# Attention scores of two heads: four small matmuls against a block-diagonal product, and four more units masked by TensorE

## The chip, the cores and the metric

The program runs on one core of one Trainium2 chip. The metric is the device time of one execution in microseconds (us). Before the change the median of three runs is 630.11 us (627.29 to 633.33). One more execution was profiled; its own time is 631.83 us, and its trace spans 630.1 us.

## The reference

Sliding-window causal attention feeds a mixture of experts that picks one expert for each token. All data is fp32.

```
B, H, S, DH = 8, 8, 576, 64          # 4608 tokens, 8 heads
scores = (q @ k^T) / sqrt(DH)        # a query sees itself and the 63 keys before it
attn   = softmax(where(0 <= rel < 64, scores, -1e9))
x      = (attn @ v) as (B, S, H*DH)  # D = 512
logits = x @ w_gate                  # E = 8 experts, F = 1024
e      = argmax(logits), or the expert of the token before where sigmoid(x @ w_local) >= 0.5
out    = softmax(logits)[e] * (relu(x @ w1[e]) @ w2[e])
```

## The kernel before, in words

**Stages.** `attention` computes x, stores it to DRAM (`xs`, L547) and computes the gate's logits on the way. `Router` works out which tokens go to which expert. `Experts.run` then takes blocks of up to 256 tokens of one expert, gathers their rows and does the two products. The Router's first part is woven into the end of attention, its second part into the first expert blocks.

**Tiling of the attention.** The 4608 tokens are nine superchunks (`sc`, 512 tokens each), the heads are four pairs (`hp`). A unit is one (sc, hp): 36 units. Head j of a pair lies on partitions 64j to 64j+63, for queries as for keys. Keys go in blocks of 64 (`WIN`), eight in a superchunk. A query sees the keys of its own block and of the one before, so each key block meets 128 queries. `scores` (L387) puts the scores of even key blocks of the superchunk on partitions 0 to 63 of a PSUM bank (c = 0) and those of the odd ones on partitions 64 to 127 (c = 1), one bank `sp[j]` for each head, 512 queries wide. Each product (L394) takes 64 rows (one head), 64 columns (64 keys) and 128 queries, or 64 at the ends. A quarter of the array holds it; the four quarters (two heads, two values of c) take turns in the code. An fp32 product appears twice in the trace, so that the 18 products of a unit are 36 matmuls and 36 weight loads there.

**What follows the scores.** ScalarE takes exp of each bank into `p` (L425), VectorE multiplies `p` with a mask (L430), except in the units in `BIASED`: there TensorE first writes a large negative number to the masked places (`bias`, `never`, L409, bf16) and adds the scores to it. `values` (L433) does 16 fp32 products (L440): 128 rows, which are the keys of two blocks, 64 columns of queries, and 65 (74 from superchunk 4 on) values of one head. VectorE divides by the sum (L445, L450).

**What sets the order.** TensorE, ScalarE and SP follow the order of the code. In the loop over the units (L479) the scores run two units ahead (`LEAD`): the body emits the scores of unit i+2, then copies of values for the next superchunk (`shift`), transposes or gate products, then the values of unit i. GpSimd and VectorE are placed by a scheduler.

**Loads.** Queries and keys lie together in DRAM (`kq`). One tile of a ring of four (`ring`, 16 KB a partition) holds both for one superchunk. `load(sc + 3, pairs)` at hp = 1 (L533) issues two DMAs of 1 MB from SP; the ring makes the first wait until the scores of superchunk sc are done. Values (`va`) are loaded two superchunks ahead at hp = 0, transposed values (`vtt`) at hp = 2. Later the same ring holds the experts' weights w1 and w2.

## Time and profile before

| what | us |
|---|---|
| median of three runs | 630.11 |
| profiled execution, its own time | 631.83 |
| its span | 630.1 |
| attention's last values begin | 133.31 |
| first expert products begin | 134.50 |

PE is the matmuls, PEld the weight loads that run beside them, DVE is VectorE, ACT ScalarE, POOL GpSimd, SP the engine that issues the loads. The profile's table of 40 slices shows PE at 70 to 90 per cent until some 110 us, and at 90 per cent or more from there nearly to the end, so that the kernel has two parts to read: the attention, in which PE has gaps, and the experts, in which it has next to none. The DMA engines show eight tenths or more in the first nine slices. Idle time of an engine that nobody waits for costs nothing, so a row says something about the time only where PE stands behind it.

### The profile page before, as it was taken

How to read it: one execution, taken by the hardware profiler on the slowest of the kernel's cores; microseconds unless marked ns; L12 is line 12 of the kernel's file. 1: busy time of each engine (PE TensorE's matmuls, PEld its weight loads, DVE VectorE, ACT ScalarE, POOL GpSimd, SP SyncE). 2: the span in 40 equal slices, each digit the busy share in tenths (PEclk: the TensorE clock that was granted, in tenths of full speed). 3: DMA queues.
4: the chain of work that ended last, by engine and by line, in shares of the span. 5: the costliest groups of instructions: out<-in, count | busy, mean ns of one | idle time of the engine just before them, and what ended most of it. 6: DMA issues, size and time to landing. Idle time of an engine off the chain costs nothing. (4 is left out here: it accounts for less than half of the span.)

```text
span 630.1 us, 15072 instructions
## 1 busy us (share of the span) xinstructions
PE 604.0 (96%) x6253; PEld 530.7 (84%) x6253; DVE 402.1 (64%) x757; ACT 200.7 (32%) x368; POOL 275.5 (44%) x261
## 2 busy tenths in 40 slices
PE   8897988999999999999999999999999999999995
PEld 7676766788889998979898889888997998989994
DVE  5667569888986867346472785183927753886730
ACT  3756655632482131203130213022211221213120
POOL 4532111532103567448165873174375765462001
PEclk9999999999999999999999999999999999999998
DMA  8999898886945566487966765678678656965501
GB/s 319 397 419 400 326 377 298 287 319 238 384 154 202 185 227 250 165 295 248 403 244 236 304 221 208 225 305 318 284 262 320 225 186 240 374 217 208 197 18 39
DMA packets 31880, 165.80 MB, mean 263 GB/s; under 512 B 10531, under 2 KB 12217, under 8 KB 22586
## 3 DMA queue, kind: packets, MB, share of 16 engines
q1 hardware_dynamic: 20394, 135.54, 57.9%
q0 software_dynamic: 11408, 29.20, 13.0%
q8 instruction: 51, 0.84, 0.5%
q14 instruction: 27, 0.22, 0.1%
HBM read 145.52 MB, written 19.59 MB: 262 GB/s over the span
## 5 line engine op out<-in xcount | busy, mean ns | idle before, releaser
L1184 POOL DMA_INDIRECT xg<-xs,g x118 | 139.1, 1179 | 46.5 <-issue 25.6
L1488 POOL DMA_INDIRECT out_dram<-y,idx x36 | 40.8, 1133 | 159.0 <-DVE y L1419 69.9
L1408 PE MATMUL hp<-ws,hs 128*128 128x256 f32 x384 | 88.9, 380 | 0.0
L1408 PEld LDWEIGHTS hp<-ws,hs 128*128 128x128 f32 x384 | 72.6, 190 | 10.9 <-issue 1.2
L1357 PE MATMUL hp<-xs,ws 128*128 128x128 f32 x672 | 79.7, 275 | 0.0
L1357 PEld LDWEIGHTS hp<-xs,ws 128*128 128x128 f32 x672 | 77.3, 192 | 0.1
L1508 PE MATMUL hp<-xt,w 128*64 128x64 f32 (+2 forms) x640 | 66.2, 276 | 0.0
L1508 PEld LDWEIGHTS hp<-xt,w 128*128 128x128 f32 (+1 forms) x640 | 60.8, 170 | 4.1 <-issue 0.7
L1419 DVE SCALAR_TENSOR_TENSOR y<-hp,pws,kept 128x256 f32<-128x256 f32 x48 | 22.1, 480 | 63.5 <-issue 38.1
L1408 PE MATMUL hp<-w,h 128*128 128x256 f32 x256 | 60.5, 379 | 0.0
L1369 DVE TENSOR_TENSOR h<-hp,keep 128x512 f32<-128x512 f32 x42 | 28.6, 690 | 44.0 <-PE hp L1357 43.2
L1357 PEld LDWEIGHTS hp<-xt,w 128*128 128x128 f32 x448 | 53.2, 192 | 2.7 <-issue 2.3
L1357 PE MATMUL hp<-xt,w 128*128 128x128 f32 x448 | 54.7, 275 | 0.0
L394 PEld LDWEIGHTS sp<-w 64*64 64x64 f32 x1296 | 39.9, 139 | 16.1 <-issue 11.5
L1408 PEld LDWEIGHTS hp<-w,h 128*128 128x128 f32 x256 | 47.3, 190 | 5.7
L394 PE MATMUL sp<-w 64*64 64x128 f32 (+1 forms) x1296 | 45.8, 272 | 5.7 <-issue 4.2
L425 ACT ACTIVATE p<-sp 128x512 f32<-128x512 f32 x72 | 39.1, 595 | 37.6 <-PE sp L394 35.2
L440 PE MATMUL xo<-vb,p 128*64 128x74 f32 (+1 forms) x576 | 45.0, 230 | 5.5 <-DVE x L450 2.2
L430 DVE TENSOR_TENSOR p<-p,mask 128x1024 f32<-128x1024 f32 x29 | 35.6, 1227 | 22.6 <-ACT p L425 22.5
L1184 POOL DMA_INDIRECT pws<-xw,gx x40 | 43.7, 1093 | 13.1 <-issue 9.8
L440 PEld LDWEIGHTS xo<-vb,p 128*64 128x64 f32 x576 | 39.2, 139 | 9.7 <-issue 4.0
L1320 DVE TENSOR_TENSOR ws<-w 128x1024 f32<-128x1024 f32 x32 | 39.1, 1224 | 11.5 <-PE hp L1408 9.6
(287 smaller groups left out, 967.3 us busy)
## 6 DMA issues: line engine op xcount, KB each, us to landing
w<-in_w_dram SPq DMA_DIRECT2D x22, 2048.0 KB, 9.4
w<-in_w1t_dram SPq DMA_DIRECT2D x20, 2048.0 KB, 8.9
w<-in_kq_dram SPq DMA_DIRECT2D x17, 1024.0 KB, 10.4
w<-in_w_dram SPq DMA_DIRECT2D x24, 512.0 KB, 8.3
xs<-x POOLq DMA_DIRECT2D x9, 1024.0 KB, 7.0
va<-in_v_dram SPq DMA_DIRECT2D x5, 1184.0 KB, 5.3
vtt<-in_vt_dram SPq DMA_DIRECT2D x5, 1024.0 KB, 6.3
va<-in_v_dram SPq DMA_DIRECT2D x3, 1040.0 KB, 14.2
```

Of the source, the lines that this page charges most:

```text
L394: nc.tensor.matmul(sp[j][c * WIN:(c + 1) * WIN, a:b], lhsT=kt[h, hp, block * WIN:(block + 1) * WIN], rhs=qt[h, hp, a:b], start=not biased, ...
L425: nc.scalar.activation(p[:, j], sp[j], Act.Exp, scale=DH ** -0.5)
L430: masked.append(nc.vector.tensor_tensor(p, p, m.to_broadcast([P, 2, SC]), op=Alu.mult))
L440: nc.tensor.matmul(xo[par * WIN:(par + 1) * WIN, j, s * VW:s * VW + n], lhsT=p[:, j, b * WIN:(b + 1) * WIN], rhs=w[:, s, 2 * hp + j, :n], ...
L1184: return self.nc.gpsimd.indirect_dma_start(out=out, out_offset=None, in_=table[:rows, :], in_offset=bass.IndirectOffsetOnAxis(ap=idx, axis=0))
L1320: self.nc.vector.tensor_tensor(o, x, y, op=sub)
L1357: mm = nc.tensor.matmul(out[:, m, :], lhsT=a[:, kk, m * P:(m + 1) * P], rhs=b[:, kk, :], start=start and m + kk == 0, stop=stop and (m, kk ...
L1369: nc.vector.tensor_tensor(o, x, y, op=add)
L1408: mm = nc.tensor.matmul(out, lhsT=a[:, m, :], rhs=b[:, m, :], start=start and m == 0, stop=stop and m == FK // 2 - 1, skip_group_check=True)
L1419: nc.vector.scalar_tensor_tensor(o, x, pw[i], y2, Alu.mult, Alu.add)
L1488: return self.nc.gpsimd.indirect_dma_start(out=self.out[:, :], out_offset=bass.IndirectOffsetOnAxis(ap=st["idx"][:, s:s + 1], axis=0), in_ ...
L1508: mm = nc.tensor.matmul(hp[a, i, :], lhsT=st["w1"][:, kk, m * P:(m + 1) * P][:, a], rhs=st["xt"][:, kk, :n], start=(kk == 0), stop=(kk == ...
```

## The change

- **Scores.** The queries of a pair of heads go into a tile whose second axis is the head: head 0's queries on partitions 0 to 63 at place 0, head 1's on partitions 64 to 127 at place 1, and zeros elsewhere. One product takes the keys of both heads (128 rows, 64 keys) and streams the queries of both places (2 x 128). The zeros keep the heads apart. A unit has 10 products, not 18. A bank `sp[i]` now holds both heads for one half (256 queries) of the superchunk, and exp goes by halves.
- **Masks.** (7, 1), (7, 3), (8, 0) and (8, 2) join `BIASED`: 11 units get their mask from TensorE, 25 from VectorE. The bias products take one half of the queries and write it for both heads.
- **Loads.** The ring is two tiles `w1` and two tiles `w2`. Keys: one `w1` tile holds two superchunks, the last superchunk's keys have a tile of their own. Queries: the two `w2` tiles take turns for even and odd superchunks, and their zeros are written once (`clear`). Queries are loaded two superchunks ahead, a pair of `hp` at a time, in two DMAs of 64 partitions each; the first two of all are issued by ScalarE. The experts' weights use `w1` and `w2` in the same turns.

TensorE, the scores of the unit (0, 2) and the first values after them, before. `sp` is the scores' bank, `w` the tile with keys and queries, `xo` the output of the values; the sizes are rows and streamed elements.

```order
L394 MATMUL sp<-w 64x128 x2
L394 MATMUL sp<-w 64x64 x2
L394 MATMUL sp<-w 64x128 x12
L394 MATMUL sp<-w 64x64 x2
L440 MATMUL xo<-vb,p 64x65
L440 MATMUL xo<-va,p 64x65
```

The same place now; `w_129` holds queries and `w_138` keys.

```order
L417 MATMUL sp<-w_129,w_138 64x2x128
L417 MATMUL sp<-w_129,w_138 64x2x64
L417 MATMUL sp<-w_129,w_138 64x2x128 x2
L417 MATMUL sp<-w_129,w_138 64x2x64 x2
L417 MATMUL sp<-w_129,w_138 64x2x128 x3
L417 MATMUL sp<-w_129,w_138 64x2x64
L465 MATMUL xo<-vb,p 64x65
L465 MATMUL xo<-va,p 64x65
```

The unit's 18 products have become 10; six of them stream 2 x 128 queries and four 2 x 64. The place among the other work is the same.

SP's loads from superchunk 2's first unit to the next superchunk's, before, with what each waits for (`DMAHW` is the landing of an earlier load, `PE` a matmul):

```order
L235 DMA va<-in_v_dram 128x2368 [waits PE_49,DMAHW3_49,Activation_49,Pool_49]
L240 DMA w<-in_kq_dram 128x2048 [waits DMAHW4_49,PE_49]
L240 DMA w<-in_kq_dram 128x2048 [waits DMAHW5_49]
L230 DMA vtt<-in_vt_dram 128x2048 [waits DMAHW6_49]
L235 DMA va<-in_v_dram 128x2368 [waits PE_49,DMAHW7_49,Activation_49,Pool_49]
```

The same stretch now:

```order
L246 DMA va<-in_v_dram 128x2368 [waits PE_49,DMAHW1_49,Activation_49,Pool_49]
L259 DMA w_129<-in_kq_dram 64x1024 [waits DMAHW2_49]
L259 DMA w_129<-in_kq_dram 64x1024 [waits DMAHW3_49]
L254 DMA w_785<-in_kq_dram 128x2048 [waits DMAHW4_49,PE_49]
L259 DMA w_129<-in_kq_dram 64x1024 [waits DMAHW5_49,PE_49]
L259 DMA w_129<-in_kq_dram 64x1024 [waits DMAHW6_49]
L241 DMA vtt<-in_vt_dram 128x2048 [waits DMAHW7_49]
L254 DMA w_785<-in_kq_dram 128x2048 [waits DMAHW0_49]
L246 DMA va<-in_v_dram 128x2368 [waits PE_49,DMAHW1_49,Activation_49,Pool_49]
```

Two loads of a superchunk's keys and queries, three superchunks ahead, have become four of queries (two superchunks ahead) and two of keys (here for superchunks 4 and 5).

The diff, without the lines on the experts' ring and the later paths:

```diff
-BIASED = [(4, 3), (5, 1), (5, 3), (6, 0), (6, 1), (6, 2), (6, 3)]
+BIASED = [(4, 3), (5, 1), (5, 3), (6, 0), (6, 1), (6, 2), (6, 3), (7, 1), (7, 3), (8, 0), (8, 2)]
...
-        ring = fast.enter_context(tc.tile_pool(name="ring", bufs=4))
+        ring = fast.enter_context(tc.tile_pool(name="ring", bufs=2))
...
+    turns = [ring.tile([P, 2, 2, 2, SC], F32, name="w2") for _ in range(2)]
+    turns.reverse()
+    for sc in range(NSC):
+        qts[sc] = turns[sc % 2]
+
+    def clear(sc, pair, hps, engines):
+        for j, e in enumerate(engines):
+            e.memset(qts[sc][j * DH:(j + 1) * DH, pair, 1 - j, hps], 0.0)
+
+    clear(0, 0, slice(0, 1), (nc.gpsimd, nc.vector))
...
             else:
-                if sc not in kqs:
-                    kqs[sc] = ring.tile([P, HP, 2, SC], F32, name="w")
-                    kts[sc], qts[sc] = kqs[sc][:, :, 0], kqs[sc][:, :, 1]
-                nc.sync.dma_start(out=kqs[sc][:, part], in_=kq[sc, :, part])
+                pair, hps = part if isinstance(part, list) else (part, slice(0, 2))
+                for j in range(2):
+                    h, e = slice(j * DH, (j + 1) * DH), nc.scalar if (sc, pair, hps.stop) == (0, 0, 1) else nc.sync
+                    e.dma_start(out=qts[sc][h, pair, j, hps],
+                                in_=kq[sc, h, 1, 2 * pair + hps.start:2 * pair + hps.stop])
...
-    load(0, [slice(0, 1), slice(1, 2), (0, H // 2), pairs[1], (H // 2, H)])
+    load(0, [[0, slice(0, 1)], slice(0, 1), slice(1, 2), [0, slice(1, 2)], (0, H // 2), pairs[1], 1, (H // 2, H)])
...
+    clear(0, 0, slice(1, 2), (nc.gpsimd, nc.vector))
+    clear(0, 1, slice(0, 2), (nc.gpsimd, nc.gpsimd))
+    clear(1, 0, slice(0, 2), (nc.gpsimd, nc.gpsimd))
...
     def scores(sc, hp):
-        qt, kt = qts[sc], kts[sc]
-        sp = [ps_s.tile([P, SC], F32, name="sp") for _ in range(2)]
+        qt, kt, half = qts[sc][:, hp // 2, :, hp % 2], kts[sc], SC // 2
+        sp = [ps_s.tile([P, 2, half], F32, name="sp") for _ in range(2)]
...
-        def one(j, c, kt, block, a, b):
-            h = slice(j * DH, (j + 1) * DH)
-            nc.tensor.matmul(sp[j][c * WIN:(c + 1) * WIN, a:b], lhsT=kt[h, hp, block * WIN:(block + 1) * WIN],
-                             rhs=qt[h, hp, a:b], start=not biased, stop=True, skip_group_check=biased)
+        def one(c, kt, block, a, b):
+            i = a // half
+            nc.tensor.matmul(sp[i][c * WIN:(c + 1) * WIN, :, a - i * half:b - i * half],
+                             lhsT=kt[:, hp, block * WIN:(block + 1) * WIN], rhs=qt[:, :, a:b],
+                             start=not biased, stop=True, skip_group_check=biased)
...
-                        nc.tensor.matmul(sp[j][c * WIN:(c + 1) * WIN, a], lhsT=unit[h], rhs=x, start=not n, stop=False,
-                                         skip_group_check=True)
-        for s in range(5):
-            for c in range(2):
-                for j in range(2):
-                    if c == 0:
-                        if s < 4:
-                            one(j, 0, kt, 2 * s, s * P, (s + 1) * P)
-                    elif s:
-                        one(j, 1, kt, 2 * s - 1, s * P - WIN, min(s * P + WIN, SC))
-                    elif sc:
-                        one(j, 1, kts[sc - 1], KB - 1, 0, WIN)
-                    else:
-                        one(j, 1, kt, 1, 0, WIN)
+                            a, w, x = first * WIN - i * half, WIN, never[h]
+                        nc.tensor.matmul(sp[i][c * WIN:(c + 1) * WIN, :, a:a + w], lhsT=unit[h],
+                                         rhs=x.rearrange("p (o q) -> p o q", o=1).to_broadcast([DH, 2, w]),
+                                         start=not n, stop=False, skip_group_check=True)
+        for b in range(KB):
+            if b % 2 == 0:
+                one(0, kt, b, b * WIN, (b + 2) * WIN)
+            lo = b * WIN
+            if b == 0:
+                one(1, *((kts[sc - 1], KB - 1) if sc else (kt, 1)), 0, WIN)
+            elif b % 2 and (lo + WIN) % half:
+                one(1, kt, b, lo, lo + 2 * WIN)
+            elif b % 2:
+                one(1, kt, b, lo, lo + WIN)
+                if b + 1 < KB:
+                    one(1, kt, b, lo + WIN, lo + 2 * WIN)
         p = pp.tile([P, 2, SC], F32, name="p")
-        for j in range(2):
-            nc.scalar.activation(p[:, j], sp[j], Act.Exp, scale=DH ** -0.5)
+        for i in range(2):
+            nc.scalar.activation(p[:, :, i * half:(i + 1) * half], sp[i], Act.Exp, scale=DH ** -0.5)
...
         if 0 < sc < NSC - 2 and hp == 0:
-            load(sc + 2, [whole])
-        if 0 < sc < NSC - 3 and hp == 1:
-            load(sc + 3, pairs)
+            load(sc + 2, [whole, 0])
+        if sc and sc % 2 == 0 and sc + 2 < NSC and hp == 1:
+            load(sc + 2, [slice(0, HP)])
+        if 0 < sc < NSC - 2 and hp == 2:
+            load(sc + 2, [1])
         if hp == 2 and sc + 2 in GATED:
             load(sc + 2, ["turned"])
+        if sc and sc % 2 == 0 and sc + 3 < NSC and hp == 3:
+            load(sc + 3, [slice(0, HP)])
```

More of the change, by code (lines that the diff above doesn't have):

```diff
@@ L148 @@
             with ExitStack() as slow:
-                ring = slow.enter_context(tc.tile_pool(name="ring2", bufs=4))
+                ring = slow.enter_context(tc.tile_pool(name="ring2", bufs=2))
                 rt = Router(slow, tc, lt, xs, tabs, ident)
@@ L160 @@
         with tc.If(if_more > 0), ExitStack() as slow:
-            ring = slow.enter_context(tc.tile_pool(name="ring3", bufs=4))
+            ring = slow.enter_context(tc.tile_pool(name="ring3", bufs=2))
             Experts(slow, tc, ring, *moe).more(slow)
@@ L211, in attention @@
     ctx.enter_context(tc.manual_schedule(engines={ET.PE, ET.Activation, ET.SP}))
-    kqs, qts, kts, vts, vas, vbs = {}, {}, {}, {}, {}, {}
+    qts, kts, vts, vas, vbs = {}, {}, {}, {}, {}
+    turns = [ring.tile([P, 2, 2, 2, SC], F32, name="w2") for _ in range(2)]
[6 more added lines that the diff above has]
+    clear(0, 0, slice(0, 1), (nc.gpsimd, nc.vector))
     def width(sc):
@@ L235, in load @@
                 nc.sync.dma_start(out=vas[sc][:, :, h], in_=src[:, :, h])
-            else:
-                if sc not in kqs:
-                    kqs[sc] = ring.tile([P, HP, 2, SC], F32, name="w")
-                    kts[sc], qts[sc] = kqs[sc][:, :, 0], kqs[sc][:, :, 1]
-                nc.sync.dma_start(out=kqs[sc][:, part], in_=kq[sc, :, part])
+            elif isinstance(part, slice):
+                if sc not in kts:
+                    if sc == NSC - 1:
+                        kts[sc] = cp.tile([P, HP, SC], F32, name="last")
+                    else:
+                        both = ring.tile([P, 2, HP, SC], F32, name="w1")
+                        kts[sc], kts[sc + 1] = both[:, 0], both[:, 1]
+                nc.sync.dma_start(out=kts[sc][:, part], in_=kq[sc, :, 0, part])
+            else:
+                pair, hps = part if isinstance(part, list) else (part, slice(0, 2))
[3 more added lines that the diff above has]
+                                in_=kq[sc, h, 1, 2 * pair + hps.start:2 * pair + hps.stop])
     late = cp.tile([1, 4], F32, name="late")
@@ L400, in scores @@
                 for c in range(2):
-                    for j in range(2):
-                        h, a = slice(j * DH, (j + 1) * DH), slice(0, SC)
-                        x = bias[h, c].rearrange("p b i q -> p (b i q)")
+                    for i in range(2):
+                        h, a, w = slice(i * DH, (i + 1) * DH), 0, half
+                        x = bias[h, c].rearrange("p b i q -> p (b i q)")[:, i * half:(i + 1) * half]
                         if n:
-                            if first >= KB or c == first % 2:
+                            if first >= KB or c == first % 2 or i != first * WIN // half:
@@ L407, in scores @@
                                 continue
-                            a, x = slice(first * WIN, (first + 1) * WIN), never[h]
-                        nc.tensor.matmul(sp[j][c * WIN:(c + 1) * WIN, a], lhsT=unit[h], rhs=x, start=not n, stop=False,
-                                         skip_group_check=True)
-        for s in range(5):
-            for c in range(2):
-                for j in range(2):
-                    if c == 0:
-                        if s < 4:
-                            one(j, 0, kt, 2 * s, s * P, (s + 1) * P)
-                    elif s:
-                        one(j, 1, kt, 2 * s - 1, s * P - WIN, min(s * P + WIN, SC))
-                    elif sc:
-                        one(j, 1, kts[sc - 1], KB - 1, 0, WIN)
-                    else:
-                        one(j, 1, kt, 1, 0, WIN)
+                            a, w, x = first * WIN - i * half, WIN, never[h]
@@ L423, in scores @@
         p = pp.tile([P, 2, SC], F32, name="p")
-        for j in range(2):
-            nc.scalar.activation(p[:, j], sp[j], Act.Exp, scale=DH ** -0.5)
+        for i in range(2):
+            nc.scalar.activation(p[:, :, i * half:(i + 1) * half], sp[i], Act.Exp, scale=DH ** -0.5)
         if biased:
@@ L461, in attention @@
     until(0, masks[0][:1, :1])
-    load(1, [pairs[0], whole, pairs[1]])
+    load(1, [pairs[0], 0, whole, pairs[1], 1])
     moves, gated, turned, old = (), None, None, None
@@ L515, in attention @@
             until(1, allr[:1, 0, 0, 0, :1])
-            load(2, [pairs[0], whole, pairs[1]])
+            load(2, [slice(0, HP), whole, 0])
             nc.sync.dma_start(out=vhs, in_=vh)
-            load(3, pairs)
+            load(3, [slice(0, HP)])
+        if i == 1:
+            load(2, [1])
         if i == 2:
@@ L521, in attention @@
                 small()
+                clear(1, 1, slice(0, 2), (nc.gpsimd, nc.gpsimd))
         if i == 2 * HP:
@@ L1256, in weights @@
                 continue
-            t = self.ring.tile([P, a * b], F32, name="w")
+            t = self.ring.tile([P, a * b], F32, name=name)
             src = w[bass.ds(e, 1)].rearrange("o p x -> (o p) x")
@@ L1720 @@
         "v": v.reshape(N, D),
-        "kq": _np.stack([by_sc(turned(i[n])) for n in "kq"], 3),
+        "kq": _np.stack([by_sc(turned(i[n])) for n in "kq"], 2),
         "v3": v3,
```

## The prediction

> **What bounds the kernel now.** I read the busy times by stretch first, then what TensorE waits for, then single score units.
>
> ```profile
> PE 604.0 (96%) x6253; PEld 530.7 (84%) x6253; DVE 402.1 (64%) x757; ACT 200.7 (32%) x368; POOL 275.5 (44%) x261
> core 0: us, PE busy (x) PEld busy (x) DVE busy (x) ACT busy (x) POOL busy (x), PEclk, DMA share, GB/s
> 0.00:14.30 14.30, 11.79 (x158) 10.37 (x158) 8.61 (x19) 4.29 (x6) 4.93 (x13) 1.00 0.85 310
> 14.30:62.00 47.70, 40.01 (x960) 33.51 (x955) 31.23 (x65) 32.41 (x51) 19.17 (x29) 1.00 1.01 405
> 62.00:105.00 43.00, 39.63 (x909) 30.86 (x912) 29.39 (x96) 25.72 (x47) 8.27 (x8) 1.00 0.93 345
> 105.00:134.50 29.50, 27.22 (x710) 23.26 (x701) 26.22 (x61) 18.28 (x33) 11.00 (x9) 1.00 0.80 273
> 134.50:630.10 495.60, 485.39 (x3535) 432.71 (x3532) 306.63 (x518) 119.97 (x232) 232.10 (x203) 0.99 0.66 240
> ```
>
> The attention ends at 134.5 us. From 14.3 us on, PE is idle in it for 47.70 - 40.01 + 43.00 - 39.63 + 29.50 - 27.22 = 13.3 us out of 120.2. The experts fill PE (485.4 of 495.6) and are not edited. So PE's own work sets the pace of both parts; what the change puts on PE in the attention moves everything behind it. What those 13.3 us wait for, by the waits of PE from 14.3 to 134.5 us:
>
> ```profile
> PE sp L394 <- issue: 4.2, 4, 1.6
> PE xo L440 <- issue: 2.9, 4, 1.4
> PE xo L440 <- DVE x L450: 2.2, 3, 1.4
> PE xo L440 <- ACT p L313: 1.2, 2, 0.7
> ```
>
> 7.1 us are "issue": nothing that the profile shows was missing, and yet a group of matmuls stops in its middle. The other 6.2 us are hand-overs, nearly all from VectorE and ScalarE. A wait for keys and queries is not among them.
>
> **A score unit now.** The timeline of PE around one unit (start, duration):
>
> ```profile
> 18.28 0.27 PE L440 MATMUL xo<-vb,p 128*64 128x65 f32 x1
> ...
> 18.39 0.22 PE L440 MATMUL xo<-vb,p 128*64 128x65 f32 x1
> ...
> 19.21 0.22 PE L440 MATMUL xo<-vb,p 128*64 128x65 f32 x1
> ...
> 19.36 1.12 PE L394 MATMUL sp<-w 64*64 64x128 f32 x36
> 20.41 0.33 PE L310 MATMUL xo<-ident,x 128*128 128x128 f32 x1
> ```
>
> The 36 matmuls take 20.41 - 19.36 = 1.05 us up to the next group, which is 29 ns each: far less than a matmul of 128 columns needs alone, because four quarters of the array work at once. The values before them (16 pairs `vb`, `va`, each pair one column half each) go at (19.21 - 18.39) / 14 = 0.059 us a pair, 0.90 ns a streamed column; there, two halves work at once.
>
> **The scores after.** A product fills all 128 rows, so only the two column halves are left to work side by side. Each half streams 2 heads x 512 queries = 1024 columns, twice for fp32: 2048. Per column I take the row of the long fp32 matmuls nearest in size, which stream 256 as six of the ten products do:
>
> ```profile
> L1508 PE MATMUL hp<-xt,w 128*128 128x256 f32 x128 | 29.0, 382 | 0.0
> ...
> 31.24 1.07 PE L323 MATMUL r<-p,wgs 128*32 128x512 f32 x8
> 32.24 1.12 PE L394 MATMUL sp<-w 64*64 64x128 f32 x36
> ```
>
> 29.0 / 128 = 0.227 us for 256, or 0.885 ns a column; 2048 x 0.885 = 1.81 us a unit. By the values' 0.90 it is 1.85. The two timeline rows bound it from below: the gate's eight matmuls stream 2 x 512 columns through each of four column strips in 32.24 - 31.24 = 1.00 us; less the 0.14 of a switch (below) that is 0.84 a column and 1.72 a unit. I take 1.81: 0.76 more than 1.05, and **+27.4 us** over 36 units. Half of the multiplications are by zero, and the array's time is the price.
>
> This holds if both halves run freely. The code's order of halves is 0, 1, 1, 0, 1, 1, 0, 1, 0, 1 with 2, 1, 2, 2, 1, 1, 2, 2, 2, 1 times 128 columns. If no matmul could begin before the one ahead of it had begun, the halves would wait for one another: stepping through it (two passes each) I get 19 steps of 128 columns, not 16, or 19/16 x 1.81 = 2.15 us. What speaks against it is the first unit with a bias:
>
> ```profile
> 74.60 0.41 PE L409 MATMUL sp<-bias,unit 64*64 64x512 bf16 x4
> 74.84 0.27 PE L394 MATMUL sp<-w 64*64 64x128 f32 x2
> 74.84 0.19 PE L409 MATMUL sp<-never,unit 64*64 64x64 bf16 x2
> ```
>
> The code emits `never` ahead of the scores, yet the scores of the other half stand ahead of it by start. So a half does not wait for its neighbour. The Trainium skill, "TensorE: Matmul & The Clock Gate", Part 3, says that matmuls are strictly first in, first out, in start as in end. Taken at its word that gives the 2.15; this row differs from it by a few nanoseconds in one place, which is why the case stays a rival.
>
> **Switches of shape.** In the timeline above, the last values start at 19.21 and the scores at 19.36, 0.15 later where 0.059 would do; the first pair of values needs 0.11 (18.28 to 18.39) where 0.059 would do. So passing between 64-row and 128-row products costs 0.09 + 0.05 = 0.14 us. Scores and values now have the same shape. Where they touch (15 times scores then values, 14 times the other way round), it goes: 29 x 0.14 = **-4.1 us**. Where bias products (64 rows) precede the scores it comes: 11 x 0.14 = **+1.5 us**. The bias of four more units costs what the row at 74.60 shows until the next start, 0.24 us each: **+1.0 us**.
>
> **The slow beginning.** PE's first units run at half speed, though PEclk reads 1.00:
>
> ```profile
> 5.01 2.39 PE L394 MATMUL sp<-w 64*64 64x128 f32 x38 [0.69 <-DMA w<-in_kq_dram]
> 7.73 1.98 PE L394 MATMUL sp<-w 64*64 64x128 f32 x34 [0.33 <-ACT p L425]
> 9.64 1.54 PE L256 MATMUL r<-ident 128*128 128x128 f32 x6
> 11.28 0.32 PE L440 MATMUL xo<-vb,p 128*64 128x65 f32 x1
> ...
> 11.38 0.32 PE L440 MATMUL xo<-vb,p 128*64 128x65 f32 x1
> ```
>
> Two units take 9.64 - 5.01 - 0.33 = 4.3 us, and a pair of values 0.10. Both units pay the 0.76 twice: **+1.5 us** beyond the sum above. So PE's work grows by 27.4 - 4.1 + 1.5 + 1.0 + 1.5 = **27.3 us**.
>
> **What may come back.** Stops by "issue" come after about 250 instructions of PE, counting weight loads:
>
> ```profile
> 34.96 0.65 PE L394 MATMUL sp<-w 64*64 64x128 f32 x10
> 36.43 0.99 PE L394 MATMUL sp<-w 64*64 64x128 f32 x26 [0.83 <-issue]
> q8 instruction: 51, 0.84, 0.5%
> ```
>
> Queue q8 moves instructions in 51 packets of 16 KB, through the DMA engines that are full in this stretch (share 1.01). I read the stops as a packet that lands late. The scores lose 36 x 16 = 576 matmuls and as many weight loads, and a packet now lasts longer on PE: fewer packets, and more time for each. Bounds: 0 to 7.1 us back; I take **-4.5**. Of the 6.2 us of hand-overs some go because VectorE, ScalarE and loads have more time while PE works; bounds 0 to 6.2, I take **-3**.
>
> **The rest.** Four masks leave VectorE:
>
> ```profile
> L430 DVE TENSOR_TENSOR p<-p,mask 128x1024 f32<-128x1024 f32 x29 | 35.6, 1227 | 22.6 <-ACT p L425 22.5
> ```
>
> 4 x 1.23 = 4.9 us of an engine that PE waits for 2.2 us in all (the row L440 <- DVE), which is inside the hand-overs: nothing more. Exp by halves has the same 512 elements; its first half can begin when half of the unit's products are done, which shortens a path that runs two units ahead of its use. The zeros add about 5 us on GpSimd (ten times the 512 elements that the first row here clears in 0.53) and little on VectorE:
>
> ```profile
> 2.05 0.53 POOL L382 MEMSET vb<- 64x520 f32 x1
> 8.84 1.49 POOL L383 COPY vb<-va 64x1040 f32<-64x1040 f32 x1 [6.27 <-DMA va<-in_v_dram]
> ```
>
> GpSimd waits 6.27 us there for a load, and this covers them; without that cover the values of the first unit would come up to 5 us late. SP now has to issue some five loads of keys and queries a superchunk, not two, and each waits for the landing of the eighth before it; at the start this can hold back superchunk 1's loads behind the first values. I put the start at **+0.5**, bounds 0 to 3. The bytes are the same. Keys and queries now come at least five units (some 17 us) ahead of use, not nine, and a load of 1 MB lands in 10:
>
> ```profile
> w<-in_kq_dram SPq DMA_DIRECT2D x17, 1024.0 KB, 10.4
> ```
>
> A load of 64 partitions is not in this trace. If it takes twice that row's time per byte, half a megabyte lands in the same 10.4 us and still in time; a gain I exclude, since PE hardly waits for loads now. The weights' ring gives the same tile back after the same use as before.
>
> **The sum:** 27.3 - 4.5 - 3 + 0.5 = +20.3 us on the profiled execution's 631.83, so 652.1. That execution is 1.7 us above the median of 630.11, which makes **650**.
>
> **Rivals.**
> The halves wait for one another (2.15 us a unit): 36 x 0.34 = 12 us on top, 662. Chance 0.12; the row at 74.84 speaks against it.
> Loads come late: the queries' lead shrinks, and SP waits in order. If each of the superchunks 2 to 8 stops PE for 2 us, it is 14 on top, 664. DMA share 1.01 speaks for it, that PE slows and so asks for less per microsecond against. Chance 0.06.
> PE is hidden: if up to 62 us the loads (share 1.01), not PE, set the pace, the 16 or so units up to there cost nothing extra. The other 20 cost 20 x 0.76 = 15, less the 7.5 that comes back and less 2.6 net of switches: about +5, 635. Against it: PE is busy 84% there and its stops are not for loads. Chance 0.05.
> Faster: the place is the score unit. If 29 ns were the price of giving out a matmul, and not of its columns, 20 matmuls of a unit would take 0.6 to 0.9 us: with 0.75, 36 x 0.30 = 11 us off, 4.1 of switches and 7.5 of waits, less the bias 2.5, 20 us in all, 610. It decides from 2048 columns in under 1.05 us, 0.51 ns each, on; the rows of L1508 and of the values show 0.89 and 0.90. Chance 0.03.
>
> **The numbers.** The forecast as summed has 0.74. Its own span: all 13.3 us of idle back and 1.72 us a unit gives 27.3 - 3.2 - 13.3 = +10.8, 641; nothing back, 1.85 a unit and 3 at the start gives 27.3 + 1.4 + 3 = +32, 662. The range of 638 to 666 holds that and most of the two slower rivals. A measurement of this kernel tells 1% (6.3 us) from no change. Faster by more than that: 0.03; within it: the hidden case and a little of the forecast's lower end, 0.06; slower: 0.91.
>
> **What would show it.** Right: the score group takes 1.75 to 1.85 us on the timeline where it took 1.05; values start without a gap behind scores; the first experts' products begin at about 155 us, not 134.5, and take the same time from there; PE's idle time in the attention falls to some 6 us, above all the stops by "issue". Wrong: a score unit at 1.1 us or below, waits of PE for the loads of keys or queries, or experts that begin late for another reason than PE's own work.

## The result and the profile after

The changed kernel takes 652.14 us (median of four runs, 649.3 to 655.97) against 629.3 us for the kernel before (four runs, 627.29 to 633.33). The ratio is 1.0359, with a 95% interval of 1.0274 to 1.0444: slower by 3.6%. The profiled execution took 649.62 us, 17.8 more than the one profiled before, and spans 647.8. The lines below are of that execution, one of the two faster ones of the four. Where two profiles of one kernel are compared, a second profile of either kernel shows how far one execution can be trusted: the attention of the kernel before ended at 134.5 us in one profile and at 132.07 in another, that of the changed kernel at 153.2 and 159.5.

The busy times of the changed kernel, first of the whole span, then by stretch (the columns as in the prediction: length, busy time and instructions of PE, PEld, DVE, ACT and POOL, PEclk, DMA share, GB/s):

```profile
PE 628.1 (97%) x5688; PEld 544.3 (84%) x5688; DVE 404.0 (62%) x755; ACT 205.3 (32%) x368; POOL 273.6 (42%) x269
...
0.00:14.30 14.30, 10.73 (x95) 8.96 (x97) 12.34 (x20) 4.51 (x6) 8.74 (x17) 1.00 0.89 255
14.30:27.20 12.90, 10.76 (x183) 9.33 (x180) 8.82 (x12) 8.73 (x13) 9.26 (x14) 1.00 1.04 327
27.20:62.00 34.80, 33.17 (x493) 25.96 (x495) 20.86 (x51) 19.28 (x30) 8.32 (x17) 0.95 1.03 301
62.00:105.00 43.00, 40.98 (x616) 30.41 (x614) 23.27 (x57) 27.04 (x43) 8.93 (x10) 1.00 1.01 344
105.00:153.20 48.20, 47.11 (x784) 36.91 (x779) 33.22 (x104) 25.70 (x44) 11.26 (x11) 1.00 0.92 301
153.20:647.80 494.60, 485.36 (x3532) 432.69 (x3532) 305.48 (x515) 120.08 (x232) 227.12 (x203) 1.00 0.65 239
```

The attention ends at 153.2 us, not 134.5: 18.7 later. What follows it takes 494.6 us where it took 495.6, so the whole loss lies in the attention. There PE's idle time from 14.3 us on is 2.14 + 1.63 + 2.02 + 1.09 = 6.9 us, against 13.3. Two columns moved that the forecast had not spoken of. The DMA engines are as busy as before (share 1.04 and 1.03) but deliver 327 and 301 GB/s where the kernel before had 405. And PEclk is 0.95 in one stretch.

What PE waited for from 14.3 to 153.2 us (total, times, longest):

```profile
PE sp L417 <- DMA w<-in_kq_dram: 2.2, 1, 2.2
PE xo L465 <- ACT p L336: 1.6, 2, 1.3
PE xo L465 <- issue: 1.3, 1, 1.3
```

Of the 7.1 us of "issue" 1.3 are left. There is one wait for queries, of 2.2 us. A score unit, on PE's timeline (start, duration):

```profile
119.92 0.23 PE L465 MATMUL xo<-va,p 128*64 128x74 f32 x1
119.97 1.91 PE L417 MATMUL sp<-w,w 128*64 128x256 f32 x20
121.69 0.23 PE L465 MATMUL xo<-vb,p 128*64 128x74 f32 x1
```

The unit occupies PE for 121.69 - 119.97 = 1.72 us, and the scores begin 0.05 after the last values: no price for a switch. This is one of the shortest units. Without the first two, which run slowly, and the one at 27.22 us (below), the 33 others take 1.72 to 1.96 us with idle time left out, 1.83 on average. In the kernel before, an undisturbed unit takes 1.05, but the 34 units after the first two average 1.16, because a unit with a stop in it takes up to 1.57 even with the stop itself left out.

The next table gives PE's time up to the first expert product by kind of work, from the start of each group to the start of the next one less the idle time between them. It was worked out from the trace, in us:

```
                     scores  values  bias  other  idle  first expert product
before                 43.8    43.2   1.8   29.9  14.4   134.5
changed kernel         69.1    39.5   4.2   29.9   8.6   153.2
difference            +25.3    -3.7  +2.4    0.0  -5.8   +18.7   (first instruction +0.4)
```

### The profile page after: what moved, and what is told of

Read it like the earlier page. It is cut to its first block, busy times and chain, and to the rows that moved or that the text cites. A ratio compares the mean times of both kernels' runs of the same rounds, so it can differ in the third digit from the quotient of the medians.

```text
span 647.8 us, 13992 instructions
## 1 busy us (share of the span) xinstructions
PE 628.1 (97%) x5688; PEld 544.3 (84%) x5688; DVE 404.0 (62%) x755; ACT 205.3 (32%) x368; POOL 273.6 (42%) x269
## 5 line engine op out<-in xcount | busy, mean ns | idle before, releaser
L1216 POOL DMA_INDIRECT xg<-xs,g x118 | 135.9, 1152 | 49.1 <-issue 25.6
L1520 POOL DMA_INDIRECT out_dram<-y,idx x36 | 40.4, 1121 | 158.4 <-DVE y L1451 69.4
L417 PE MATMUL sp<-w,w 128*64 128x256 f32 (+1 forms) x648 | 66.6, 351 | 3.9 <-DMA w<-in_kq_dram 3.9
L417 PEld LDWEIGHTS sp<-w,w 128*64 128x64 f32 x648 | 49.2, 142 | 20.1 <-issue 10.4
L450 ACT ACTIVATE p<-sp 128x512 f32<-128x512 f32 x72 | 42.8, 598 | 44.5 <-PE sp L417 42.9
L1216 POOL DMA_INDIRECT pws<-xw,gx x40 | 42.0, 1049 | 14.5 <-issue 7.3
L455 DVE TENSOR_TENSOR p<-p,mask 128x1024 f32<-128x1024 f32 x25 | 31.8, 1273 | 24.8 <-ACT p L450 24.7
L465 PE MATMUL xo<-vb,p 128*64 128x74 f32 (+1 forms) x576 | 42.6, 226 | 3.2 <-ACT p L336 1.6
L1402 ACT ACTIVATE h<-h 128x512 f32<-128x512 f32 x42 | 26.3, 630 | 60.0 <-DVE h L1401 60.0
## 6 DMA issues: line engine op xcount, KB each, us to landing
w<-in_kq_dram SPq DMA_DIRECT2D x36, 256.0 KB, 14.4
w<-in_kq_dram SPq DMA_DIRECT2D x6, 1024.0 KB, 15.2
```

The lines of the kernel that those rows point to most:

```text
L417: nc.tensor.matmul(sp[i][c * WIN:(c + 1) * WIN, :, a - i * half:b - i * half], lhsT=kt[:, hp, block * WIN:(block + 1) * WIN], rhs=qt[:, :, ...
L450: nc.scalar.activation(p[:, :, i * half:(i + 1) * half], sp[i], Act.Exp, scale=DH ** -0.5)
L455: masked.append(nc.vector.tensor_tensor(p, p, m.to_broadcast([P, 2, SC]), op=Alu.mult))
L465: nc.tensor.matmul(xo[par * WIN:(par + 1) * WIN, j, s * VW:s * VW + n], lhsT=p[:, j, b * WIN:(b + 1) * WIN], rhs=w[:, s, 2 * hp + j, :n], ...
L1216: return self.nc.gpsimd.indirect_dma_start(out=out, out_offset=None, in_=table[:rows, :], in_offset=bass.IndirectOffsetOnAxis(ap=idx, axis=0))
L1402: nc.scalar.activation(o, x if y is None else o, Act.Relu)
```

## The experiments

The runs were made on three chips, and each time stands beside runs of the kernel before on its own chip: 642.53 us beside the product only, loads only, half loads and short rows; 629.46 beside the repeat of the changed kernel, head by head, queries first and wide queries; 630.73 beside the others. Where a single run was made, it is one look without an interval.

### The price of the products: product only

`e5_product_only` is the kernel before with the large product, the bias products and the exp by halves that go with it; its loads and its list of masks are untouched. The queries of the pair stream twice instead of once each beside zeros:

```diff
-            nc.tensor.matmul(sp[j][c * WIN:(c + 1) * WIN, a:b], lhsT=kt[h, hp, block * WIN:(block + 1) * WIN],
-                             rhs=qt[h, hp, a:b], start=not biased, stop=True, skip_group_check=biased)
+            nc.tensor.matmul(sp[i][c * WIN:(c + 1) * WIN, :, a - i * half:b - i * half],
+                             lhsT=kt[:, hp, block * WIN:(block + 1) * WIN],
+                             rhs=qt[:, a:b].rearrange("p (o q) -> p o q", o=1).to_broadcast([P, 2, b - a]),
+                             start=not biased, stop=True, skip_group_check=biased)
```

> The kernel before with the products alone: one product of 128 rows and 2 x 128 columns, exp by halves, old loads, old ring, old masks list. The queries are streamed twice in place of the block-diagonal pair, so that each score is the sum of both heads' (that part of the computation is changed). Theory A: score group 1.73 to 1.89 us, attention's end at 150 to 152 us (before: 134.5), total 645 to 649. Theory B, loads as the cause: total 632 or below.

Measured: 649.03 us (646.16 to 651.17) against 642.53, a ratio of 1.0108 (1.0085 to 1.0131). The experts may get other tokens here, so the attention's end says more: 143.3 us. A second profile of the same kernel beside a second one of the kernel before, on another chip, was taken for that reason.

> The products alone once more (each score is the sum of both heads', so that other experts may be picked and the part behind the attention isn't the same work; the attention's end is the measure). Theory A with the idle time that came back the first time: first expert product 9 to 11 us later than in the kernel before of this call, score group 1.73 to 1.89 us, stops by issue under 1 us. If the first result was the chip's: 15 us later or more.

> The kernel before, profiled once more as the measure for this call. All theories: first expert product at 132 to 136 us, stops by issue of some 7 us in the attention, each ending 1.3 to 1.6 us after an instruction packet has landed.

They gave 639.09 and 629.01 us, with the attention ending at 142.45 and 132.07: +10.4. The first pair, on two chips, gives 143.3 - 134.5 = +8.8. Two stretches of the first profile, and what PE waited for in its attention:

```profile
14.30:62.00 47.70, 46.77 (x741) 37.34 (x739) 31.72 (x67) 32.04 (x50) 17.33 (x28) 1.00 1.02 410
62.00:105.00 43.00, 42.30 (x625) 30.90 (x623) 26.35 (x90) 24.93 (x42) 6.63 (x7) 1.00 0.87 321
```

```profile
PE xo L442 <- ACT p L313: 0.9, 1, 0.9
PE xo L442 <- issue: 0.7, 2, 0.3
```

PE is idle for 0.93 + 0.70 us in these 90.7 us, where the kernel before was idle for 7.69 + 3.37. Worked out as in the table, for the first and the second pair of profiles, the scores cost 22 to 23 us more (43.8 to 65.8 and 42.7 to 65.5), the bias 1 more and the values 3 to 4 less, some 20 us in all, and 10 us of idle time vanish (14.4 to 4.3, and 14.6 to 4.2). So the product alone costs about 10 us, because PE's gaps close for the most part behind it.

### The price of the loads: loads only, half loads, short rows

`e1_loads_only` is the changed kernel with the old products and the old list of masks. Its loads, tiles, zeros and ring are the new ones:

```diff
-BIASED = [(4, 3), (5, 1), (5, 3), (6, 0), (6, 1), (6, 2), (6, 3), (7, 1), (7, 3), (8, 0), (8, 2)]
+BIASED = [(4, 3), (5, 1), (5, 3), (6, 0), (6, 1), (6, 2), (6, 3)]
...
+            nc.tensor.matmul(sp[j][c * WIN:(c + 1) * WIN, a:b], lhsT=kt[h, hp, block * WIN:(block + 1) * WIN],
+                             rhs=qt[h, j, a:b], start=not biased, stop=True, skip_group_check=biased)
```

> The changed kernel with the old products: the new loads, query tiles and ring stay, but scores are made by 64-row products for one head at a time as before, and the masks are those of before. Theory A (the column stream of the 128-row products sets the time; the loads cost only the start): the attention ends some 5 us later than before, near 139 us, total 633 to 636, and the score group is back at 1.05 us. Theory B (the loads of 64 partitions lower the rate of the DMA engines from 405 to some 310 GB/s and set the time as well): some 46 MB of the attention at 320 GB/s need 145 us, PE waits for loads in its trace, total 638 to 643. If the loads alone were the cause of the whole loss, it would be 652.

Measured: 666.64 us (664.21 to 668.14) against 642.53, ratio 1.0359 (1.0333 to 1.0384). Without one new product, the new loads lose as much as the whole change. Its attention ends at 151.1 us, 19.1 later than that of the short rows (below, 132.0) on the same chip; what follows takes 6.9 us longer (515.2 against 508.3), and nothing here explains that part. Two stretches, PE's first two waits, and one of the stops with the clock behind it:

```profile
14.30:62.00 47.70, 37.51 (x782) 30.97 (x780) 26.93 (x58) 24.71 (x39) 19.31 (x29) 0.86 1.02 299
62.00:105.00 43.00, 37.43 (x849) 29.67 (x845) 24.52 (x58) 27.83 (x47) 9.51 (x10) 0.99 0.98 352
```

```profile
PE sp L417 <- issue: 9.2, 7, 3.4
PE xo L463 <- issue: 5.4, 4, 2.2
```

```profile
36.78 0.91 PE L417 MATMUL sp<-w,w 64*64 64x128 f32 x9 [3.36 <-issue]
```

```profile
36.78:40.20 3.42, 3.42 (x45) 2.73 (x49) 1.34 (x2) 1.88 (x4) 0.26 (x1) 0.50 1.00 373
```

299 GB/s at a DMA share of 1.02; 14.6 us of stops by "issue" in these two rows, where the kernel before had 7.1; and after the longest one PE runs at half its clock (PEclk 0.50 in the last row; the trace has it from 35.9 to 42.7 us, 6.8 in all). To tell which property of the new loads does it, two kernels change only the loads of the kernel before. `e6_half_loads` cuts each load of 1 MB into two of 64 partitions, with the same rows of 8 KB:

```diff
-                nc.sync.dma_start(out=kqs[sc][:, part], in_=kq[sc, :, part])
+                for h in (slice(0, DH), slice(DH, P)) if part == pairs[0] or part == pairs[1] else (slice(0, P), ):
+                    nc.sync.dma_start(out=kqs[sc][h, part], in_=kq[sc, h, part])
```

> The kernel before, each 1 MB load of keys and queries issued as two loads of 64 partitions with the same rows of 8 KB; nothing else. If loads of 64 partitions lower the rate: DMA share stays 1.0 from 14.3 to 62 us, but at 300 to 350 GB/s in place of 405, and the attention ends 3 to 8 us later (635 to 640). If the size of the rows does it: 405 GB/s and 630.

`e7_short_rows` cuts it into two of 128 partitions with rows of 4 KB, as the queries have them now:

```diff
-                nc.sync.dma_start(out=kqs[sc][:, part], in_=kq[sc, :, part])
+                for hp in range(part.start, part.stop):
+                    nc.sync.dma_start(out=kqs[sc][:, hp:hp + 1], in_=kq[sc, :, hp:hp + 1])
```

> The kernel before, each 1 MB load of keys and queries issued as two loads of 128 partitions with rows of 4 KB; nothing else. If the size of the rows lowers the rate: 300 to 350 GB/s from 14.3 to 62 us and 635 to 640. If the 64 partitions do it: 400 GB/s and 630.

Measured, one look each: 680.21 us for the half loads and 642.12 for the short rows, beside 642.53 for the kernel before. The same two stretches of the half loads, and below them PE's waits up to the end of its attention at 172.4 us:

```profile
14.30:62.00 47.70, 32.13 (x666) 26.79 (x666) 19.50 (x34) 19.27 (x31) 11.98 (x18) 0.86 1.02 247
62.00:105.00 43.00, 31.78 (x609) 24.75 (x613) 20.91 (x45) 22.39 (x35) 9.63 (x15) 0.89 1.02 287
```

```profile
PE xo L441 <- issue: 12.6, 5, 3.1
PE sp L395 <- issue: 9.1, 4, 3.7
PE xo L441 <- ACT p L314: 5.8, 2, 3.5
PE sp L395 <- DMA w<-in_kq_dram: 4.1, 3, 2.3
```

And of the short rows:

```profile
14.30:62.00 47.70, 40.64 (x948) 33.32 (x949) 32.48 (x67) 31.41 (x50) 18.05 (x29) 1.00 1.02 409
62.00:105.00 43.00, 38.63 (x917) 30.72 (x919) 32.02 (x105) 27.66 (x49) 10.27 (x9) 1.00 0.96 358
```

Short rows and twice the number of loads cost nothing: 409 GB/s, the attention ends at 132.0. It is the 64 partitions: 247 GB/s with the engines fully busy, although loads of 128 partitions (the values) run among them. The Trainium skill, "SBUF — State Buffer", section "Door 1: The DMA port swizzle (why `[64,N]` ≈ `[32,N]`)", says that a transfer's rate depends on how many of the 16 ports into the memory its partitions reach, and that partitions 0 to 63 reach eight. The row agrees in direction; it shows 247 and 287 GB/s and not half of the 405, and which port a packet took no run here shows.

Why a slower rate stops PE where it waits for no data, queue q8 shows. It moves instructions in packets of 16 KB, and their number follows PE's: 51 packets for the 12,506 matmuls and weight loads before, 47 for 11,376 in the changed kernel, 52 for 12,816 head by head (below). So we take them for PE's. From the trace of the kernel before and of the loads-only kernel, the landing of such packets and the end of the next stop of PE by "issue" (us):

```
before       35.01 -> 36.43   41.50 -> 42.92   47.68 -> 49.11   60.88 -> 62.16   91.65 -> 93.02
loads only   18.66 -> 19.95   26.71 -> 28.23   35.19 -> 36.78   50.05 -> 51.55   57.42 -> 58.94
```

A stop ends 1.3 to 1.6 us after a packet has landed, each time, and the stops are 252 to 256 instructions of PE apart, or a multiple of that (504 to 508, 1,270 to 1,274). So the traces bear out the prediction's reading of "issue": PE runs out of instructions, and the packet with the next ones comes through the same full DMA engines as the loads.

### Both together: head by head, queries first, wide queries

The changed kernel was timed again on the chip of the next three, so that they have something to stand beside:

> The changed kernel once more, as the measure for the others of this call. All theories: about 1.036 of the kernel before, the first expert product at 153 us.

Measured: 654.44 us (651.25 to 656.21) against 629.46, ratio 1.0384 (1.0349 to 1.042). The profiled execution was the slowest of the four, 656.21. In it PE is idle for 13.4 us up to the first expert product, hardly less than the 14.4 before, because more loads came late: it waits 2.8 us for queries, 2.7 for ScalarE, which waits for values, and 2.2 for transposed values.

`e4_head_by_head` cuts each product of the changed kernel in two, one for each place of the queries. The columns streamed stay, the instructions double:

```diff
-            nc.tensor.matmul(sp[i][c * WIN:(c + 1) * WIN, :, a - i * half:b - i * half],
-                             lhsT=kt[:, hp, block * WIN:(block + 1) * WIN], rhs=qt[:, :, a:b],
-                             start=not biased, stop=True, skip_group_check=biased)
+            for j in range(2):
+                nc.tensor.matmul(sp[i][c * WIN:(c + 1) * WIN, j, a - i * half:b - i * half],
+                                 lhsT=kt[:, hp, block * WIN:(block + 1) * WIN], rhs=qt[:, j, a:b],
+                                 start=not biased, stop=True, skip_group_check=biased)
```

> The changed kernel with each of its 10 products cut into two, one for each head's columns: the same 128 rows, the same columns in all, the same loads, but 20 products, so that a unit has 40 matmuls and 40 weight loads in the trace in place of 20. Theory A (columns price the unit): score group 1.75 to 1.95 us as in the changed kernel. Rival (the number of matmuls prices it): 2.3 us and more. Theory C (a stop of PE is an instruction packet that lands late; 250 instructions then last 4.8 us in place of 6.6): stops by issue of 4 to 10 us in the attention where the changed kernel has 1.3, total 3 to 8 us above the changed kernel; without C, the same as the changed kernel.

Measured: 658.70 us (657.24 to 659.87), ratio 1.0461 (1.0436 to 1.0486), 4.3 us above the changed kernel beside it. PE's waits in its attention by "issue":

```profile
PE xo L466 <- issue: 2.9, 2, 2.6
...
PE sp L418 <- issue: 1.7, 2, 1.3
PE r L363 <- issue: 0.8, 1, 0.8
...
PE sp L434 <- issue: 0.3, 1, 0.3
```

The stops are back at 5.7 us, from 1.5 in the profile of the changed kernel on this chip, while the scores take 72.2 us and not 69.4. That is 0.08 us a unit for 20 more matmuls: the columns are the price, and the number of instructions shows in the stops.

`e8_queries_first` moves the second pair of superchunk 1's keys and queries ahead of its values:

```diff
-    load(1, [pairs[0], 0, whole, pairs[1], 1])
+    load(1, [pairs[0], 0, pairs[1], 1, whole])
```

> The changed kernel with superchunk 1's second pair of queries and keys loaded ahead of its values; nothing else. Theory D (late queries stop PE at 25 us and the stop halves PE's clock for the next 3.4 us): both go, 3 to 4 us below the changed kernel. Rival (another load of the full queue is late in its place): within 1 us of it.

Measured: 650.28 us (648.08 to 654.07), ratio 1.0355 (1.0313 to 1.0397). The place where the changed kernel waits for queries and then runs at half clock, in the changed kernel (timeline, then PEclk in three stretches):

```profile
27.22 3.08 PE L417 MATMUL sp<-w,w 128*64 128x256 f32 x20 [2.17 <-DMA w<-in_kq_dram]
30.23 1.59 PE L333 MATMUL xo<-ident,x 128*128 128x128 f32 x8
...
43.61 1.09 PE L333 MATMUL xo<-ident,x 128*128 128x128 f32 x8
```

```profile
27.90:31.30 3.40, 3.40 (x20) 2.69 (x17) 0.33 (x1) 1.53 (x3) 0.00 (x0) 0.50 1.08 287
31.30:34.70 3.40, 3.35 (x57) 2.65 (x55) 1.79 (x3) 1.14 (x2) 0.72 (x1) 1.00 1.02 335
```

and the same unit with the queries first, the waits behind it, and its clock:

```profile
25.96 1.91 PE L417 MATMUL sp<-w,w 128*64 128x256 f32 x20
...
28.99 1.09 PE L333 MATMUL xo<-ident,x 128*128 128x128 f32 x8 [1.12 <-ACT p L336]
...
33.02 1.05 ACT L394 COPY vb<-va 64x1040 f32<-64x1040 f32 x1 [2.44 <-DMA va<-in_v_dram]
...
35.16 0.27 PE L465 MATMUL xo<-vb,p 128*64 128x65 f32 x1 [2.25 <-ACT p L336]
```

```profile
27.20:62.00 34.80, 31.22 (x490) 24.13 (x484) 21.14 (x51) 21.38 (x34) 10.88 (x20) 1.00 1.03 323
```

The wait for queries at this unit is gone and the clock stays at 1.00. But PE's idle time from 27.2 to 62 us is not less: 34.80 - 31.22 = 3.6 us, against 1.6 in the changed kernel. Now the values land later: ScalarE waits for them before its copies (L394, then L336), and PE waits 1.12 and 2.25 us for ScalarE. With a full queue, what is moved back comes late in its turn. The medians differ by 4.2 us in favour of this order, but the intervals overlap, so the size stays uncertain. The rate is still 323 GB/s.

`e9_wide_queries` loads the queries' tiles whole, 128 partitions with their zeros from DRAM (9.4 MB more), and so needs no clearing:

```diff
-                for j in range(2):
-                    h, e = slice(j * DH, (j + 1) * DH), nc.scalar if (sc, pair, hps.stop) == (0, 0, 1) else nc.sync
-                    e.dma_start(out=qts[sc][h, pair, j, hps],
-                                in_=kq[sc, h, 1, 2 * pair + hps.start:2 * pair + hps.stop])
+                e = nc.scalar if (sc, pair, hps.stop) == (0, 0, 1) else nc.sync
+                e.dma_start(out=qts[sc][:, pair, :, hps], in_=qz[sc, :, pair, :, hps])
```

> The changed kernel with the queries' tiles loaded whole, zeros from DRAM included: loads of 128 partitions, no clearing of tiles, 9.4 MB more to load. Theory B (loads of 64 partitions are what lowers the rate, and what the changed kernel loses beside its products): DMA rate back at 390 GB/s and above until 60 us, start as before, first expert product at 146 to 148 us, ratio to the kernel before 1.015 to 1.025. If the bytes or the order of the loads do it: 1.036 or more.

Measured: 645.70 us (644.85 to 646.6), ratio 1.0265 (1.0242 to 1.0289). Its interval lies wholly below that of the changed kernel beside it (1.0349 to 1.042): 8.7 us less, although it loads more bytes. Its stretches:

```profile
14.30:62.00 47.70, 44.22 (x709) 35.80 (x707) 30.21 (x62) 29.91 (x47) 19.07 (x30) 1.00 1.02 415
62.00:105.00 43.00, 42.30 (x634) 30.86 (x629) 24.70 (x71) 25.91 (x42) 6.18 (x7) 1.00 1.01 420
105.00:148.80 43.80, 42.73 (x723) 34.00 (x719) 29.76 (x89) 24.51 (x42) 11.28 (x11) 1.00 0.94 330
```

415 and 420 GB/s, no stop by "issue", the clock at full; one wait for queries of 1.9 us is left at 19.5. So the loads of 64 partitions (with the clearing, which this kernel leaves out too) cost some 8.7 us in the changed kernel beyond what the extra bytes cost here, and the remaining 16 are the product's, the masks', the start's and those bytes'.

### The masks alone, and later loads

`e3_masks_only` is the kernel before with the four new units in its list of masks:

```diff
-BIASED = [(4, 3), (5, 1), (5, 3), (6, 0), (6, 1), (6, 2), (6, 3)]
+BIASED = [(4, 3), (5, 1), (5, 3), (6, 0), (6, 1), (6, 2), (6, 3), (7, 1), (7, 3), (8, 0), (8, 2)]
```

> The kernel before with the longer list of units masked by TensorE alone. PE gets four times 0.24 us of bias products, VectorE loses four masks of 1.23 us. By the prediction's terms: between 1 us slower (nothing comes back) and 1 us faster (the waits for VectorE between 105 and 110 us, 1.8 us, go): 0.998 to 1.002. A rival in which VectorE bounds the end of the attention: 0.993 or less.

Measured: 631.77 us (12 runs) against 630.73 (23 runs), ratio 1.0009 (0.9992 to 1.0026). No difference can be told.

`e10_later_loads` asks whether the kernel before gets its stops back if its loads are issued later, so that fewer stand ahead of the instruction packets:

```diff
+        if i == 3:
             load(3, pairs)
...
-        if 0 < sc < NSC - 3 and hp == 1:
+        if 0 < sc < NSC - 3 and hp == 3:
             load(sc + 3, pairs)
```

> The kernel before with keys and queries of superchunk sc+3 loaded at hp = 3 in place of hp = 1, and superchunk 3's after the fourth unit in place of the first: less of the loads queued early, the same bytes. Theory C (late instruction packets behind full DMA queues stop PE): some of the 7.1 us of stops between 20 and 62 us go, total 1 to 4 us faster, 0.994 to 0.999. If the queues stay full until 62 us anyway: 1.000. If keys and queries are late in their place: 1.003 and more.

Measured: 631.13 us (12 runs), ratio 1.0002 (0.9982 to 1.0022). In its profile 8.3 us of stops by "issue" are left, and from 14.3 to 62 us the engines are as busy as before (share 1.00, 406 GB/s), so putting off these loads did not empty them. No version was faster than the kernel before.

## Why the prediction was right, and where it was not

**Sign and size.** Forecast 650 with 638 to 666, measured 652.14. On the profiled execution the sum was +20.3 us, measured +17.8. The reading that PE's own work sets the pace of the attention held, and the experts took the same time behind it (494.6 for 495.6 us).

**Score products, +27.4, and the slow beginning, +1.5.** Measured +25.3 by the table, with the half clock at 28 us inside it, for 28.9. The price of a unit after the change was right, 1.83 us on average for 1.81; the shortest show 1.72, the lower bound from the gate's rows, 0.84 ns a column. Two things beside it were mis-sized. The unit before was taken at 1.05, which is an undisturbed one; the average was 1.16, so that some 0.11 x 34 = 3.7 us beyond the idle time of the stops went away too. And the slow beginning cost nothing more than it did before: the first two units took 12.17 - 6.39 = 5.78 us and not 4.3, which is 1.5 for both, where the forecast had 3.0 (0.76 for each among the products, and 1.5 on top). The spacing of PE's matmuls halves at about 10.7 us there, inside the second unit, at about 13.5 in the kernel before and between 6 and 7 in its second profile, so the length of this beginning differs between executions.

**Switches, -4.1 and +1.5, and the bias, +1.0.** The scores follow values without a gap, and the values lose 3.7 us in the table. Of these some 0.9 belong to the slow beginning (the values of the first unit took 1.93 us before and 0.98 now), so that the switches gave about 2.8 for 4.1. Bias with its switches came to +2.4 for 2.5.

**All of PE's work.** +25.3 - 3.7 + 2.4 = +24.0 (other work 0.0) for 27.3.

**What comes back, -4.5 and -3.** Idle time up to the first expert product fell by 5.8 us for 7.5, and stops by "issue" from 7.1 to 1.3. The cause of these stops was the one given, a packet of instructions that lands late: each stop ends 1.3 to 1.6 us after a landing, and cutting the products in two brings 5.7 us of them back at the same columns. But the agreement of the sum is partly luck. PE's work was forecast 3.3 us too high and the idle time that comes back 1.7 too high, and the two errors offset each other in part. The product alone wins back 10 us of idle time, 2.5 more than forecast; the loads then take some of that again, 4 us of it in one profile of the changed kernel and 9 in the other (idle time 4.3, then 8.6 and 13.4).

**"The rest": the step that failed.** The forecast put the start at +0.5 us with bounds of 0 to 3, and said of a load of 64 partitions that even at twice the time per byte it would come in time, half a megabyte in 10.4 us. A quarter of a megabyte took 14.4 us (the first row below), the loads came too late more than once, and they did more harm than that. Waits of PE for queries were among the forecast's own signs of being wrong. At the start, the first scores had to wait for queries:

```profile
6.39 5.85 PE L417 MATMUL sp<-w,w 128*64 128x256 f32 x40 [1.70 <-DMA w<-in_kq_dram]
```

They begin at 6.39 us, 1.4 later than before. Then come the stop of 2.17 us before 27.22 and the half clock behind it, which makes the unit take 30.23 - 27.22 = 3.01 us where the next ones of its kind take 1.84 to 1.91, and the eight transposes of L333 0.5 longer: 1.4 + 2.2 + 1.6 = 5.2 us at the start alone. Over the whole kernel the wide queries put the price of these loads, with the clearing, at 8.7 us. The working went wrong in taking the landing of one load for the question. That landing did grow, but what counted was the rate of the full engines, which fell from 405 to about 300 GB/s for everything behind them:

```profile
w<-in_kq_dram SPq DMA_DIRECT2D x36, 256.0 KB, 14.4
...
w<-in_kq_dram SPq DMA_DIRECT2D x6, 1024.0 KB, 15.2
```

A megabyte of keys on all 128 partitions, which the change does not cut, now lands in 15.2 us instead of 10.4. The half loads show the price without any cover: +37.7 us in one look. In the changed kernel most of it is covered: at about the same rate its stops by "issue" are 1.3 us in one profile and 1.5 in the other, where the loads-only kernel has 14.6, since a packet of instructions lasts longer on PE. That is why the parts do not add up: loads alone +3.6%, product alone +1.1%, both +3.6 to 3.8%.

**The rivals.** The halves waiting for one another (2.15 us a unit) is out: 1.72, and 1.96 at most at the full clock. The Trainium skill, "TensorE: Matmul & The Clock Gate", Part 3, has matmuls start in strict order; taken at its word this order of products would need the 2.15, so the measurement decides against that reading of it. Loads that come late happened, though not as 2 us in each superchunk: a stop for queries of 2.2 and 2.5 us in the two profiles of the changed kernel, and in the second one also a stop for values (2.7 us, through ScalarE) and one for transposed values (2.2 us, before the gate's products). The hidden case was half right: with loads of full width most of PE's idle time takes the products in, and only about 10 of the 20 us that they add show. It was wrong that the loads set the pace, since PE was the one that stayed busy. The faster case is out: the 20 matmuls cost their columns.

**What stays open.** How the 16 us of the wide queries divide among product, masks, zeros that are streamed and start was not measured one by one. That a packet waits behind the loads on one DMA engine is inferred from its landing times and from the effect of rate and instruction count; a run in which the loads leave the instruction packets' engine free was not made. The kernel before was not profiled on the chip of the loads-only kernel, and what that kernel loses behind the attention has no cause here.

## What to carry to other kernels

Before filling an array's quarters with zeros, count the columns that stream: here four quarters at work on half the rows beat one product of full height, and the number of instructions saved was worth only the stops that they caused. A change of layout that cuts a load to 64 partitions has to be priced at the rate of the full queue and not at the landing of that one load, and whatever shares the DMA engines pays it, PE's instructions among it. Where a bound resource has gaps, test the new work alone: here 10 of PE's 14 us of gaps closed behind it, so that 20 us of added work cost 10.

## What was not expected of the hardware

**64 partitions.** From 14.3 to 62 us the kernels with loads of 64 partitions move 247 to 327 GB/s at a DMA share of 1.02 to 1.04, where those with loads of 128 partitions alone move 405 to 415 at 1.01 to 1.02, with rows of 4 KB as with rows of 8 KB.

**The clock.** A stop of 2.17 us was enough: from 27.9 to 31.3 us PE ran at a PEclk of 0.50, while the kernel before had stops of up to 1.6 us in its attention without it. In the loads-only kernel a stop of 3.36 us brought 6.8 us at half clock. But the length of one stop does not decide it. The clock stayed at 1.00 after a stop of 2.52 us in the second profile of the changed kernel (ended at 27.82 us) and after the one of 2.25 with the queries first, and the kernel with the later loads ran at half clock although PE had not stopped for longer than 1.07 us since its first matmul:

```profile
16.66:20.07 3.41, 3.41 (x66) 3.21 (x58) 1.83 (x2) 1.28 (x3) 2.03 (x4) 0.50 1.04 409
```

What decides was not tested. The Trainium skill, "TensorE: Matmul & The Clock Gate", Part 1, gives about 3.4 us of work until the clock comes back, and the changed kernel's 3.4 us at half clock agree, while the 6.8 are twice that; its rule of thumb in the section on oscillation, that gaps above about 3.4 us are to be avoided, is too generous by the 2.17.

**Clearing on GpSimd beside VectorE.** The zeros slow the masks that VectorE builds beside them, by the timeline of the changed kernel:

```profile
2.41 4.91 POOL L222 MEMSET w<- 64x512 f32 x5
...
4.13 4.22 DVE L305 TENSOR_SCALAR mask<-p,rowf 64x512 f32<-64x512 f32 x4
```

and of the kernel before:

```profile
2.89 1.78 DVE L282 TENSOR_SCALAR mask<-p,rowf 64x512 f32<-64x512 f32 x4
```

and of the wide queries, which clear nothing:

```profile
2.89 1.78 DVE L303 TENSOR_SCALAR mask<-p,rowf 64x512 f32<-64x512 f32 x4
```

Four builds take 4.22 us where they took 1.78 and take 1.78 again without the clearing. The five clearings take 0.98 each where the one ahead of the masks took 0.52. The forecast had priced this at little on VectorE. Whether PE paid for it is not settled: its first scores are released by the load of queries (the row at 6.39), and the first values follow other work of PE without a gap, but no run took the clearing away by itself.
